# Attention and two MLPs on one core: first output operand split among the last pairs, fourteen early weight loads, batch 1 on the later batches' path

## The chip, the core and the metric

The kernel runs on one core of a Trainium2 chip. The metric is the device time of one execution, in microseconds (us). The core's engines run side by side: PE multiplies matrices, DVE and ACT do elementwise work, POOL and SP here mostly issue DMAs (transfers between DRAM and the on-chip buffers). Each engine works through its own instructions in the order in which they were written, and waits on semaphores for the others.

## What is computed

Cut to what matters (B = 8 batches, 8 heads, 576 positions, head width 64, 32 packed queries; both MLPs are 4608 x 512 -> 2048 -> 512):

```
p_packed = sm_attn(p, k, v)                  # 32 packed queries attend to 576 positions
x = sm_attn(q, p_packed, p_packed)           # 576 positions attend to the 32 packed rows
h = x @ w_in;  g = where(h >= 1, h, where(h <= -1, 0, (h + 1)**2 / 4));  y = g @ w_out
h = y @ w2_in; out = silu(h) @ w2_out
```

## The kernel before, in words

Every large product is made of three matmuls on high and low halves of the operands (`PASSES`), so an operand that PE reads is first cast on ACT (the high half) and subtracted on DVE (the low half). In `pair_split` these are L789 (ACT CAST) and L790 (DVE).

**First half: attention and first MLP.** Each of 8 batches is worked through in 32 steps (16 for each half of its tokens); a step is six matmuls of the first product (L662, `ps_h`), activation work on ACT (L671, L672, L681) and DVE (L677, L687), and twelve matmuls of the second product (L697, `ps_y`). Between the steps stand the attention jobs of the next batch: s1 (scores of the packed queries, lines 272 and 283), pp (the packed rows), s2 (scores of all positions against the packed rows) and wp (the packed rows multiplied into the weights w_in, so that attention and first MLP become one product). Batches 0 and 1 make s2 with 36 matmuls of 64 columns (L417), its maxima and differences straight from PSUM (L428, L430) and its transposes on PE (L454, with an eviction L474 and L476), and wp with 4 matmuls of 64 rows by 512 columns for each of two halves (L563). Batches 2 to 7 pack heads onto smaller array tiles: s2 is 16 matmuls in 64x32 tiles (L486, L497) and its transposes run on DVE (L511 STREAM_TRANSPOSE); wp is 16 matmuls in 64x32 tiles (L575). The raw weights of batch 0 and 1's time are converted on DVE by L156 and L157, `raw` and `w`, beside the steps.

**Second half: second MLP.** It runs in 6 blocks. A block has 56 h units (`h_product`, L829: six matmuls of 128x384 each) and then 56 o units (`o_product`, L881). Products are combined as in Winograd's scheme, 7 products for 8: the h units come in 8 pairs p, seven products j each, and sums of PSUM banks (`c_sum`, L850, DVE) and `c_silu` (L860, ACT) make four results, c11, c12, c21 and c22. When two pairs are there, `t_sum` (L869, DVE) makes the differences t1 to t4. The o units take the operands c11, t2, c21, t3, t1, t4, c22 in that order (`OPERAND`, j = 0 to 6), each in four tiles h = 0 to 3, and `o_split` (through `pair_split`) cuts each tile into halves four units before its first use. The weights of both products, summed beforehand and kept in DRAM, come as one tile of 256 KB a unit (`load_a`, L776, on SP's queue), in a ring of 9 tiles.

**The order.** All is put into one list, `events`, with a number (steps or units) as its key, and is written out sorted by it. `unit_h` and `unit_o` number the units of the second MLP, `bu` puts work behind a unit, and `load_a` for unit n is put 3 units ahead of it for the first nine and 8.6 units ahead for the rest. Before the second MLP starts, the last results of the first one must be stored to DRAM (L712, `y_dram`) and read back in other tiles (L784, `yr`); these transfers share SP's queue with the weights.

## Time and profile before

| what | value |
|---|---|
| median of 3 runs | 1478.59 us (1477.93 to 1478.86) |
| the profiled execution's own time | 1477.16 us |
| its span in the trace | 1475.4 us |
| PE busy | 1448.3 us, 98% of the span |
| DVE, ACT, POOL busy | 966.4, 781.8, 85.1 us |
| granted PE clock, mean | 0.999 |

The span is the time between the first and the last instruction in the trace; 1.76 us of the execution lie around it. In the rows below, an engine's idle time is given with what ended it, as `[0.37 <-DVE g L790]`: 0.37 us, ended by DVE's instruction of line 790 that made a tile g. Tiles are named without their numbers there. PEld is PE's loading of weights, SPq is SP's issuing of DMAs.

### The profile page before, as it was taken

The numbers are of one execution on the slowest core, as the hardware profiler recorded it, in microseconds if no ns is written. First come the engines' busy times: TensorE is split into PE (matmuls) and PEld (weight loads), VectorE is DVE, ScalarE is ACT, GpSimd is POOL, SyncE is SP. The second block draws the span as 40 slices with busy tenths as digits, with TensorE's granted clock in tenths as the row PEclk, the third lists the DMA queues.
The fourth block names the chain that finished last, engine by engine and source line by source line (L and its number), as shares of the span: only waits on it lengthen the run. The fifth ranks groups of instructions, "written<-read, shape, count | busy, mean of one in ns | idle before, by whom it ended". The sixth has DMA issues, their size and how long they took to land.

```text
span 1475.4 us, 28405 instructions
## 1 busy us (share of the span) xinstructions
PE 1448.3 (98%) x10534; PEld 1376.5 (93%) x10534; DVE 966.4 (66%) x1807; ACT 781.8 (53%) x1621; POOL 85.1 (6%) x132
## 2 busy tenths in 40 slices
PE   8999999999999999999999999999999999999998
PEld 6788998989899898999999999999999999999998
DVE  5887576675867758586637756755764774675664
ACT  4776667676676666667643533533542461362342
POOL 1430000000000000000000000000000000000000
PEclk9999999999999999999999999999999999999999
DMA  9563455646464654544338789789789889888886
GB/s 337 184 234 128 158 175 190 220 156 228 157 217 160 198 172 168 202 167 160 112 115 277 239 296 296 238 283 308 240 271 319 251 250 313 268 248 286 251 245 222
DMA packets 196505, 329.82 MB, mean 224 GB/s; under 512 B 30608, under 2 KB 83856, under 8 KB 196368
## 3 DMA queue, kind: packets, MB, share of 16 engines
q1 hardware_dynamic: 186896, 294.98, 61.8%
q0 software_dynamic: 9472, 33.04, 6.5%
q8 instruction: 84, 1.38, 0.4%
q14 instruction: 53, 0.43, 0.1%
HBM read 274.33 MB, written 53.61 MB: 222 GB/s over the span
## 4 chain that ended last, share of the span: by engine, by line
PE 84%; DVE 7%; ACT 2%; issue 1%; DMA 1%; SPq 0%; DVEq 0%; ACTq 0%
PE ps_y L697 24%; PE ps_h L829 23%; PE ps_o L881 21%; PE ps_h L662 12%; PE ps_wp L575 2%; DVE gt L869 1%; PE ps_pp L366 1%; DVE g L790 1%; DVE u L677 1%; DVE g L687 1%; DVE raw L156 1%; ACT g L789 1%; PE ps_wp L563 0%; DVE w L157 0%; PE ps_s L272 0%
## 5 line engine op out<-in xcount | busy, mean ns | idle before, releaser
L697 PE MATMUL ps_y<-g,w_o 128*128 128x288 f32 x3072 | 458.0, 298 | 1.7 <-POOL g L687 1.1
L697 PEld LDWEIGHTS ps_y<-g,w_o 128*128 128x128 f32 x3072 | 420.9, 188 | 33.4 <-ACT u L671 10.1
L881 PE MATMUL ps_o<-g,a2r 128*128 128x384 f32 x2016 | 355.0, 335 | 8.0 <-DVE g L790 8.0
L881 PEld LDWEIGHTS ps_o<-g,a2r 128*128 128x128 f32 x2016 | 348.9, 188 | 13.2 <-DVE g L790 13.2
L829 PE MATMUL ps_h<-y,a2r 128*128 128x384 f32 x2016 | 351.7, 334 | 2.7 <-DMA a2r<-a_dram 2.7
L829 PEld LDWEIGHTS ps_h<-y,a2r 128*128 128x128 f32 x2016 | 349.4, 188 | 3.3 <-issue 2.2
L662 PE MATMUL ps_h<-a,wp 128*128 128x288 f32 x1536 | 245.8, 296 | 2.0 <-DVE u L677 1.1
L677 DVE SCALAR_TENSOR_TENSOR u<-ps_h,u 128x288 f32<-128x288 f32 x256 | 116.1, 455 | 167.3 <-ACT u L672 166.8
L662 PEld LDWEIGHTS ps_h<-a,wp 128*128 128x128 f32 x1536 | 217.7, 188 | 5.9 <-DVE u L677 2.2
L671 ACT ACTIVATE u<-ps_h,half 128x288 f32<-128x288 f32 x256 | 128.2, 501 | 172.9 <-PE ps_h L662 153.7
L860 ACT ACTIVATE gs<-c 128x384 f32<-128x384 f32 x144 | 75.7, 526 | 136.1 <-DVE c L850 136.1
L850 DVE TENSOR_TENSOR c<-ps_h,u 128x384 f32<-128x384 f32 x144 | 79.6, 556 | 60.3 <-PE ps_h L829 50.9
L672 ACT ACTIVATE u<-u 128x288 f32<-128x288 f32 x256 | 113.8, 445 | 8.1
L687 DVE TENSOR_TENSOR g<-u,g 128x288 fp32r<-128x288 f32 x240 | 108.7, 453 | 1.6 <-ACT g L681 1.6
L681 ACT CAST g<-u 128x288 fp32r<-128x288 f32 x256 | 106.7, 417 | 0.5 <-PE ps_y L697 0.3
L790 DVE TENSOR_TENSOR g<-gs,g 128x768 fp32r<-128x768 f32 x96 | 88.4, 952 | 15.7 <-ACT g L789 15.5
L845 ACT COPY p<-ps_h 128x384 f32<-128x384 f32 x48 | 23.1, 482 | 118.6 <-PE ps_h L829 116.1
L789 ACT CAST g<-gs 128x768 fp32r<-128x768 f32 x96 | 75.6, 832 | 12.8 <-PE ps_o L881 9.4
L790 DVE TENSOR_TENSOR g<-gt,g 128x768 fp32r<-128x768 f32 x72 | 65.4, 950 | 0.0
L850 DVE TENSOR_TENSOR os<-ps_o,u 128x384 f32<-128x384 f32 x36 | 19.4, 557 | 65.2 <-PE ps_o L881 65.2
L860 ACT ACTIVATE gs<-ps_h 128x384 f32<-128x384 f32 x48 | 23.5, 492 | 72.3 <-PE ps_h L829 72.3
L913 POOL DMA_DIRECT2D out<-os x40 | 21.5, 540 | 674.4 <-ACT os L906 337.2
(131 smaller groups left out, 1123.1 us busy)
## 6 DMA issues: line engine op xcount, KB each, us to landing
a2r<-a_dram SPq DMA_DIRECT2D x336, 256.0 KB, 3.4
a2r<-o_dram SPq DMA_DIRECT2D x336, 256.0 KB, 3.1
win<-win_dram POOLq DMA_DIRECT2D x48, 512.0 KB, 4.2
raw<-w_in SPq DMA_DIRECT2D x32, 512.0 KB, 7.8
raw<-w_out SPq DMA_DIRECT2D x32, 512.0 KB, 7.2
a_dram<-a2w SPq DMA_DIRECT2D x56, 256.0 KB, 3.1
o_dram<-a2w SPq DMA_DIRECT2D x56, 256.0 KB, 2.7
y_dram<-ysb SPq DMA_DIRECT2D x36, 288.0 KB, 2.5
```

The costliest lines, as they stand in the source:

```text
L662: nc.tensor.matmul(ps[:, :HB], w[:, i, o:o + P], a2[:, k, g, :], start=(n == 0), stop=(n == 3 * NG - 1))
L671: nc.scalar.activation(u, h_ps[s][:, :HB], AF.Relu, bias=half, scale=0.5)
L672: nc.scalar.activation(u, u, AF.Square)
L677: nc.vector.scalar_tensor_tensor(u, h_ps.pop(s)[:, :HB], 1.0, u, op0=ALU.max, op1=ALU.min)
L681: nc.scalar.copy(g[:, 0], u_t[s])
L687: eng.tensor_tensor(g[:, 1], u_t.pop(s), g[:, 0].bitcast(F32), op=ALU.subtract)
L697: nc.tensor.matmul(acc["y"][d][:, :HB], w[:, i, d * P:(d + 1) * P], g[:, k], start=(first and n == 0), stop=(last and n == 2),)
L790: nc.vector.tensor_tensor(lo, src, hi.bitcast(F32), op=ALU.subtract)
L829: nc.tensor.matmul(ps, w[:, x, a * P:(a + 1) * P], b_t[i, j][k][:, a], start=(n == 0 and j in FIRST), stop=(n == 3 * KH - 1), skip_group_c ...
L850: nc.vector.tensor_tensor(t, bk[*key, b][:, :TH], sb[key, other], op=ALU.add)
L860: nc.scalar.activation(gs(*key, name), src, AF.Silu)
L881: nc.tensor.matmul(ps, w[:, x, d * P:(d + 1) * P], g[k][:, p % 2], start=(p == 0 and n == 0 and j in FIRST), stop=(p == NPR - 1 and n == 2 ...
```

## The change

It has three parts.

1. `o_split` of the first operand (j = 0, c11) goes from four units ahead of its use to ten, for h = 0 to 3 less p // 4 (p = 0, 2, 4, 6), that is among the h units of the last pairs. The four `t_sum` of the last pair go behind unit `unit_o(i, 0, 2)` and the three after it, one each. A c11 tile is kept until t1 has been made from it.
2. The first fourteen weight tiles, not nine, come from the big pool, and their loads are written 0.4 units apart from four units ahead of the first h unit.
3. Batch 1 uses the code of batches 2 to 7 in s1, s2, the transposes and wp, with its weights taken from on-chip tiles (`win_t[1, f, g] = w_in_t[g, f]`), and its wp jobs start two steps sooner.

```diff
         def pp_mm(g):
-            vs = [... if b >= 2 and g == 0 else v_t.pop((b, i)) for i in (range(2) if b >= 2 else (g,))]
+            vs = [... if b >= 1 and g == 0 else v_t.pop((b, i)) for i in (range(2) if b >= 1 else (g,))]
...
-                w = win_t[f, j // 2][:, j % 2]
+                w = win_t[b, f, j // 2][:, j % 2]
...
-            ] if b < 2 else [
+            ] if b < 1 else [
                 [J(s1_tiles), J(s1_8), J(s1_end8)],
...
-            [[J(wp, f, g) for g in range(NG)] if b < 2 else [J(wp8, f)], [J(wp_out, f, g) for g in range(NG)]]
+            [[J(wp, f, g) for g in range(NG)] if b < 1 else [J(wp8, f)], [J(wp_out, f, g) for g in range(NG)]]
...
     def store_win(f, g):
+        win_t[1, f, g] = w_in_t[g, f]
         nc.sync.dma_start(win_dram[f, g], w_in_t[g, f])
...
-    RING = 9
+    RING, FIRST_A = 9, 5
...
     def load_a(n, src):
-        if n < RING:
+        if n < RING + FIRST_A:
             t = big.tile([P, 2, KH * P], F32R, tag="big", name="a2r")
...
         nc.vector.tensor_tensor(dst, gs_t[i, h, x], gs_t[i, h, y], op=ALU.subtract)
+        if name == "t1" and (i, 0, h) in go_t:
+            gs_t.pop((i, h, "c11"))
...
     def o_split(i, j, h):
-        go_t[i, j, h] = pair_split(gs_t.pop((i, h, OPERAND[j])), "g2")
+        key = i, h, OPERAND[j]
+        go_t[i, j, h] = pair_split(gs_t[key], "g2")
+        if j or (i, h, "t1") in gs_t:
+            gs_t.pop(key)
...
-    G = dict(pf1=4, pb1=18, w1=2, pf=2, pb=16, ...)
+    G = dict(pf1=4, pb1=18, w1=0, pf=2, pb=16, ...)
...
                 if p % 2:
                     for x, name in enumerate(("t1", "t2", "t3", "t4")):
-                        bu(b + 14 + x // 2, 20 + x % 2, t_sum, i, p // 2, name)
+                        n = unit_o(i, 0, 2) + x if p == NPR - 1 else b + 14 + x // 2
+                        bu(n, 20 + x % 2, t_sum, i, p // 2, name)
...
                     if p % 2 == 0:
-                        bu(n - 4, 5, o_split, i, j, p // 2)
+                        bu(n - (4 if j else 10 - p // 4), 5, o_split, i, j, p // 2)
...
-                ev(K0 + n - (3 if n < RING else RING - 0.4) + 0.39, load_a, n, src)
+                ev(K0 + (n * 0.4 - 4 if n < RING + FIRST_A else n - RING + 0.4) + 0.39, load_a, n, src)
```

In the order's rows below a line stands for one instruction (or as many as "x3" says): line, operation, tile written <- tiles read. Lines of the new kernel are two or three lower than those of the old one.

**DVE where the first block's h units end and its o units begin.** `gs` are results c of two pairs, `gt` differences, `g2` the low halves that the o units read. Of before (gs_10323, gs_10484 and gs_10646 are the c11 tiles h = 1, 2, 3; gt_10286 is t2 of h = 0):

```order
L850 TENSOR_TENSOR c_10722<-ps_h2_10629,u2_10636 128x384
L850 TENSOR_TENSOR c_10734<-ps_h2_10588,u2_10622 128x384
L790 TENSOR_TENSOR g2_10738<-gs_10323,g2_10737 128x768
L850 TENSOR_TENSOR c_10749<-ps_h2_10600,u2_10636 128x384
L790 TENSOR_TENSOR g2_10765<-gs_10484,g2_10764 128x768
L869 TENSOR_TENSOR gt_10776<-gs_10751,gs_10646 128x768
L869 TENSOR_TENSOR gt_10778<-gs_10697,gt_10776 128x768
L790 TENSOR_TENSOR g2_10789<-gs_10646,g2_10788 128x768
L869 TENSOR_TENSOR gs_10751<-gs_10697,gs_10751 128x768
L869 TENSOR_TENSOR gt_10793<-gs_10724,gt_10778 128x768
L790 TENSOR_TENSOR y2_10804<-yr_10158,y2_10803 128x768
L790 TENSOR_TENSOR g2_10816<-gt_10286,g2_10815 128x768
```

And now (gs_10488 and gs_10650 are c11 of h = 2 and 3; gt_10290 is t2 of h = 0):

```order
L848 TENSOR_TENSOR c_10697<-ps_h2_10592,u3_10673 128x384
L848 TENSOR_TENSOR c_10707<-ps_h2_10604,u3_10687 128x384
L788 TENSOR_TENSOR g2_10712<-gs_10488,g2_10711 128x768
L848 TENSOR_TENSOR c_10723<-ps_h2_10619,u2_10626 128x384
L848 TENSOR_TENSOR c_10734<-ps_h2_10633,u2_10640 128x384
L788 TENSOR_TENSOR g2_10739<-gs_10650,g2_10738 128x768
L848 TENSOR_TENSOR c_10750<-ps_h2_10592,u2_10626 128x384
L848 TENSOR_TENSOR c_10761<-ps_h2_10604,u2_10640 128x384
L867 TENSOR_TENSOR gt_10792<-gs_10763,gs_10650 128x768
L788 TENSOR_TENSOR y2_10803<-yr_10164,y2_10802 128x768
L867 TENSOR_TENSOR gt_10806<-gs_10709,gt_10792 128x768
L788 TENSOR_TENSOR g2_10817<-gt_10290,g2_10816 128x768
```

The four splits of c11 now stand ahead of the last sums c, two of them further up than these rows, and the first split of t2 stands behind two of the last pair's differences and not behind four.

**SP where the second MLP starts.** `a2r` are the weight tiles. Of before (a2r_10152 is unit 7's, a2r_10156 unit 13's and a2r_10166 unit 8's):

```order
L776 DMA a2r_10069<-a_dram_100 128x512
L776 DMA a2r_10095<-a_dram_100 128x512
L776 DMA a2r_10099<-a_dram_100 128x512
L776 DMA a2r_10120<-a_dram_100 128x512
L776 DMA a2r_10124<-a_dram_100 128x512
L712 DMA y_dram_99<-ysb_10129 128x2x288
L712 DMA y_dram_99<-ysb_10139 128x2x288
L776 DMA a2r_10152<-a_dram_100 128x512
L776 DMA a2r_10156<-a_dram_100 128x512
L784 DMA yr_10158<-y_dram_99 128x2x384
L776 DMA a2r_10166<-a_dram_100 128x512
L776 DMA a2r_10169<-a_dram_100 128x512
```

And now:

```order
L774 DMA a2r_10021<-a_dram_100 128x512
L774 DMA a2r_10035<-a_dram_100 128x512
L774 DMA a2r_10055<-a_dram_100 128x512
L774 DMA a2r_10059<-a_dram_100 128x512
L774 DMA a2r_10073<-a_dram_100 128x512
L774 DMA a2r_10087<-a_dram_100 128x512
L710 DMA y_dram_99<-ysb_10139 128x2x288
L710 DMA y_dram_99<-ysb_10149 128x2x288
L782 DMA yr_10164<-y_dram_99 128x2x384
L774 DMA a2r_10173<-a_dram_100 128x512
L774 DMA a2r_10183<-a_dram_100 128x512
L774 DMA a2r_10193<-a_dram_100 128x512
```

All fourteen loads stand ahead of the two stores of `y_dram`, and behind the first `yr` follows unit 14's.

**PE at batch 1's first wp.** `ps_wp` and `ps_s2` are PSUM tiles of wp and s2; g_1326 is one of the tokens' second half, g_1152 the last of their first half. Of before:

```order
L697 MATMUL ps_y_1283<-g_1326,w_o_11_1276 128x288 x3
L697 MATMUL ps_y_1284<-g_1326,w_o_11_1276 128x288 x3
L697 MATMUL ps_y_1285<-g_1326,w_o_11_1276 128x288 x3
L697 MATMUL ps_y_1286<-g_1326,w_o_11_1276 128x288 x3
L417 MATMUL ps_s2_1361<-pp1_89,qt_1112 64x64 x16
L563 MATMUL ps_wp_1378<-w_in_0_0_242,pp1_89 64x512 x2
L563 MATMUL ps_wp_1381<-w_in_1_0_309,pp1_89 64x512 x2
L662 MATMUL ps_h_1393<-a2_358,wp_0_3_1166 128x288 x3
L662 MATMUL ps_h_1393<-a2_358,wp_1_3_1161 128x288 x3
```

And now:

```order
L660 MATMUL ps_h_1244<-a2_358,wp_0_3_1180 128x288 x3
L660 MATMUL ps_h_1244<-a2_358,wp_1_3_1175 128x288 x3
L572 MATMUL ps_wp8_1253<-w_in_0_0_242,pp1_89 32x512
L572 MATMUL ps_wp8_1254<-w_in_0_0_242,pp1_89 32x512
L572 MATMUL ps_wp8_1253<-w_in_0_0_242,pp1_89 32x512
L572 MATMUL ps_wp8_1254<-w_in_0_0_242,pp1_89 32x512
L572 MATMUL ps_wp8_1253<-w_in_1_0_309,pp1_89 32x512
L572 MATMUL ps_wp8_1254<-w_in_1_0_309,pp1_89 32x512
L572 MATMUL ps_wp8_1253<-w_in_1_0_309,pp1_89 32x512
L572 MATMUL ps_wp8_1254<-w_in_1_0_309,pp1_89 32x512
L695 MATMUL ps_y_914<-g_1152,w_o_7_812 128x288 x3
L695 MATMUL ps_y_915<-g_1152,w_o_7_812 128x288 x3
```

The first wp has moved from behind the first s2 to ahead of the last step of the tokens' first half, with 20 rows of the tokens' second half now between it and the first s2; it is eight rows, the two banks in turn, in place of two rows of two. DVE follows it there:

```order
L685 TENSOR_TENSOR g_1197<-u_1167,g_1197 128x288
L156 TENSOR_SCALAR raw_949<-raw_949 128x512
L157 SCALAR_TENSOR_TENSOR w_1287<-raw_949 128x512
L675 SCALAR_TENSOR_TENSOR u_1297<-ps_h_1244,u_1297 128x288
L140 TENSOR_TENSOR wp_0_0_1304<-ps_wp8_1253,wp_0_0_1304 128x512
L140 TENSOR_TENSOR wp_1_0_1307<-ps_wp8_1254,wp_1_0_1307 128x512
L685 TENSOR_TENSOR g_1263<-u_1216,g_1263 128x288
L156 TENSOR_SCALAR raw_1171<-raw_1171 128x512
L157 SCALAR_TENSOR_TENSOR w_1330<-raw_1171 128x512
L685 TENSOR_TENSOR g_1357<-u_1219,g_1357 128x288
```

Of before the two `wp` rows stood behind the first s2's maxima and differences (L428, L430):

```order
L156 TENSOR_SCALAR raw_1140<-raw_1140 128x512
L157 SCALAR_TENSOR_TENSOR w_1390<-raw_1140 128x512
L687 TENSOR_TENSOR g_1343<-u_1272,g_1343 128x288
L677 SCALAR_TENSOR_TENSOR u_1400<-ps_h_1333,u_1400 128x288
L428 TENSOR_REDUCE m2_1410<-ps_s2_1361 128x16
L430 TENSOR_TENSOR e2_1412<-ps_s2_1361,m2_1410 128x512
L140 TENSOR_TENSOR wp_0_0_1414<-ps_wp_1378,wp_0_0_1414 128x512
L140 TENSOR_TENSOR wp_1_0_1417<-ps_wp_1381,wp_1_0_1417 128x512
```

The two rows L140 have moved up by ten rows, ahead of three conversions of raw weights. In place of L428 and L430 there are now two STREAM_TRANSPOSE.

## Rows read from the trace of the kernel before

**Rows 1.** The page: shares of the chain that ended last, by engine.
```profile
PE 84%; DVE 7%; ACT 2%; issue 1%; DMA 1%; SPq 0%; DVEq 0%; ACTq 0%
```

**Rows 2.** Waits over the whole span: engine, line, releaser: us, times, longest us.
```profile
PE ps_o L881 <- DVE g L790: 8.0, 12, 1.1
...
PE ps_h L829 <- DMA a2r<-a_dram: 2.7, 2, 1.9
```

**Rows 3.** Chain of waits, second MLP: start us, us, what, matmuls.
```profile
818.31 2.09 PE ps_o L881 x12
...
878.78 58.24 PE ps_h L829 x336
...
997.48 54.09 PE ps_h L829 x312
```

**Rows 4.** Timeline at the second block's boundary: start, us, what [idle before].
```profile
937.51 0.96 DVE L790 TENSOR_TENSOR g<-gs,g 128x768 fp32r<-128x768 f32 x1 [0.85 <-ACT g L789]
938.38 0.55 DVE L850 TENSOR_TENSOR c<-ps_h,u 128x384 f32<-128x384 f32 x1
...
940.25 0.96 DVE L790 TENSOR_TENSOR g<-gs,g 128x768 fp32r<-128x768 f32 x1 [1.31 <-ACT g L789]
...
943.99 2.36 PE L881 MATMUL ps_o<-g,a2r 128*128 128x384 f32 x12 [0.37 <-DVE g L790]
...
946.46 0.95 DVE L790 TENSOR_TENSOR g<-gt,g 128x768 fp32r<-128x768 f32 x1
...
947.47 3.74 PE L881 MATMUL ps_o<-g,a2r 128*128 128x384 f32 x20 [1.12 <-DVE g L790]
```

**Rows 5.** Chain of waits where the second MLP starts: start us, us, what.
```profile
760.97 0.02 issue
...
763.41 4.58 DMA a2r<-a_dram
```

**Rows 6.** Timeline of SP there (the DMA issues).
```profile
760.62 1.17 SPq L712 DMA_DIRECT2D y_dram<-ysb  x2
761.84 0.98 SPq L776 DMA_DIRECT2D a2r<-a_dram  x2
```

**Rows 7.** Timeline of PE through batch 1's jobs.
```profile
108.14 1.37 PE L417 MATMUL ps_s<-pp,qt 128*64 128x64 f32 x29
...
109.52 1.88 PE L563 MATMUL ps_wp<-w_in,pp 128*64 128x512 f32 x7
...
113.45 1.03 PE L662 MATMUL ps_h<-a,wp 128*128 128x288 f32 x6 [0.36 <-DVE e L430]
...
119.09 0.60 PE L454 MATMUL ps_tr<-ident,e 128*128 128x128 f32 x4
```

**Rows 8.** The same jobs of a later batch, timeline of PE.
```profile
195.34 1.09 PE L486 MATMUL ps_s<-qt,pp 64*32 64x512 f32 x16
...
198.94 0.43 PE L497 MATMUL ps_s2e<-qte,pp 128*32 128x64 f32 x16
...
209.06 1.09 PE L575 MATMUL ps_wp<-win,pp 64*32 64x512 f32 x16
```

**Rows 9.** Stretches: start:end, length, busy PE PEld DVE ACT POOL, clock, DMA.
```profile
98.60:113.50 14.90, 13.90 (x119) 12.29 (x117) 14.10 (x21) 9.93 (x22) 6.87 (x6) 1.00 0.68 232
113.50:165.00 51.50, 51.50 (x413) 45.99 (x414) 31.62 (x75) 29.83 (x71) 1.09 (x2) 1.00 0.48 164
253.00:341.00 88.00, 88.00 (x799) 81.11 (x798) 60.42 (x147) 59.76 (x142) 4.75 (x9) 1.00 0.60 202
```

**Rows 10.** Timeline of DVE in batch 1's first stretch.
```profile
104.45 1.60 DVE L157 SCALAR_TENSOR_TENSOR w<-raw 128x512 uint32<-128x512 uint32 x1
...
111.91 0.68 DVE L428 TENSOR_REDUCE m<-ps_s 128x16 f32<-128x512 f32 x1
...
113.22 1.28 DVE L140 TENSOR_TENSOR wp<-ps_wp,wp 128x512 fp32r<-128x512 f32 x2
```

**Rows 11.** Timeline of DVE, the same job of a later batch.
```profile
197.53 1.30 DVE L511 STREAM_TRANSPOSE e<-ps_s 128x512 f32<-128x512 f32 x2
```

More of the change, by code (lines that the diff above doesn't have):

```diff
@@ L214, in load_k, with q_tiles @@
                 kq_t["ke", b] = t
-    def q_tiles(b):
-        if b:
-            return [[(2 * i * P, P), ((2 * i + 1) * P, P)] for i in range(SC // 2)] + [[(SC * P, ST)]]
+    def q_tiles():
         return [x for t in (0, HB) for x in ([(t, P), (t + P, P)], [(t + 2 * P, HB - 2 * P)])]
@@ L231, in load_q @@
     def load_q(b, i):
-        parts = q_tiles(b)[i]
+        parts = q_tiles()[i]
         n = sum(x[1] for x in parts)
@@ L350, in pp_mm @@
         def pp_mm(g):
-            vs = [v_t[b, i] if b >= 2 and g == 0 else v_t.pop((b, i)) for i in (range(2) if b >= 2 else (g,))]
+            vs = [v_t[b, i] if b >= 1 and g == 0 else v_t.pop((b, i)) for i in (range(2) if b >= 1 else (g,))]
             et, ett = st.pop(("eta", g)), st["etb"]
@@ L358, in pp_mm @@
                     rows = slice(h * NP, (h + 1) * NP)
-                    head = 2 * h + g if b >= 2 else h
+                    head = 2 * h + g if b >= 1 else h
                     va, vb = vs[head // 4]
@@ L374, in pp_norm @@
             for g in range(NG):
-                if b >= 2:
+                if b >= 1:
                     nc.vector.memset(t[:, g, 1 - g], 0.0)
@@ L393, in pp_out @@
             ps = st.pop("pptr")[:, :NG * P]
-            if b < 2:
+            if b < 1:
                 nc.vector.tensor_copy(pp.rearrange("p j m -> p (j m)"), ps)
@@ L402, in att_jobs @@
         W2 = NJ * N2
-        tiles = q_tiles(b)
+        tiles = q_tiles()
         def s2(i):
@@ L412, in s2 @@
                     for j in range(NJ):
-                        if b < 2:
+                        if b < 1:
                             dst = ps[r0:r1, c * W2 + j * N2:c * W2 + (j + 1) * N2]
@@ L579, in wp8 @@
             for e in range(2):
-                win_t.pop((f, e))
+                win_t.pop((b, f, e))
                 st["wp", f, e] = banks[e]
@@ L623, in back @@
         def back(every=4, only=None):
-            if b >= 2:
+            if b >= 1:
                 return back8
@@ L641, in store_win, with load_win @@
     def store_win(f, g):
+        win_t[1, f, g] = w_in_t[g, f]
         nc.sync.dma_start(win_dram[f, g], w_in_t[g, f])
-    def load_win(f, g):
+    def load_win(b, f, g):
         t = big.tile([P, 2, FW], F32, tag="big", name="win")
         nc.gpsimd.dma_start(t, win_dram[f, g])
-        win_t[f, g] = t
+        win_t[b, f, g] = t
     h_ps, u_t, g_t, acc, y_t = {}, {}, {}, {}, {}
@@ L913, in o_sum @@
                 eng.dma_start(out[r:r + P, t, i * TH:(i + 1) * TH], sb.pop(((i, 0, d), name)))
-    G = dict(pf1=4, pb1=18, w1=2, pf=2, pb=16, pw=21, lw=3, lk=4, lv=-1, lq=6, ai=34, ad=25, bev=4, oraw=1)
+    G = dict(pf1=4, pb1=18, w1=0, pf=2, pb=16, pw=21, lw=3, lk=4, lv=-1, lq=6, ai=34, ad=25, oraw=1)
     starts = {b: (0,) if b else (0, KF // 2) for b in range(B)}
@@ L1085, in plan_back @@
         def plan_back(b, n):
-            if b >= 2:
-                for g in range(NG + 1):
-                    at(n - G['lq'] + min(g, 1), load_q8, b, g)
-                slots(n, jobs[b][1]())
-                return
-            for i in range(3):
-                at(n - G['lq'] + G['bev'] * i, load_q, b, i)
-            slots(n, jobs[b][1](G['bev']))
+            for g in range(NG + 1):
+                at(n - G['lq'] + min(g, 1), load_q8, b, g)
+            slots(n, jobs[b][1]())
         jobs = {b: att_jobs(b) for b in range(1, B)}
@@ L1098, in attention_then_two_mlps @@
         for f in range(NF):
+            for g in range(NG):
+                at(KF + 4 * f + G['w1'] - 0.05, store_win, f, g)
             slots(KF + 4 * f + G['w1'], jobs[1][2][f])
-            for g in range(NG):
-                at(KF + 4 * f + G['w1'] + 0.05, store_win, f, g)
         for b in range(2, B):
@@ L1108, in attention_then_two_mlps @@
                 for g in range(NG):
-                    at(n - G['lw'], load_win, f, g)
+                    at(n - G['lw'], load_win, b, f, g)
                 slots(n, jobs[b][2][f])
```

## The prediction

> **What bounds the kernel now.** I read the chain of waits first: PE holds 84% of it and DVE 7% [rows 1], so the kernel is bound by PE and what can be won on the second half is the time in which PE stands still. The list of waits names the two places where it does so there: PE waits for the low halves of operands at L790, 8.0 us in 12 cases, and for the first weight tiles, 2.7 us in 2 cases [rows 2]. In the chain a block's h units run 58.24 us without a break, 336 matmuls, or 0.1733 us each and 1.04 us for a unit of six. The o units have as many matmuls of the same shape, yet those of the second block start at 937.02 (878.78 + 58.24) and end at 997.48: 60.46 us [rows 3]. So 2.22 us go at the boundary of a block, and the boundary of the first one reads alike (818.31 to 878.78, 60.47). The first half is bound by PE too in its steady part: a later batch's stretch is 88.00 us with PE busy for 88.00 of them. Batch 1 differs early: from 98.6 to 113.5 PE works 13.90 of 14.90 us and DVE 14.10, so there DVE is the bound; from 113.5 on PE is busy throughout, 51.50 of 51.50, with DVE at 31.62 [rows 9].
>
> **Part 1, the boundary of a block.** Before, DVE takes the second split of c11 at 937.51 and the third at 940.25, and before each it had stood idle for its ACT cast (0.85 and 1.31 us); between them stands one of the last sums (938.38). The fourth comes behind two differences of the last pair, and PE waits for it at 943.99, having been idle for 0.37. Then come two more differences, a split of y, and only then the split of t2's first tile, at 946.46; PE waits again, to 947.47, idle for 1.12 [rows 4]. Those two idles are 1.49 of the 2.22; the rest is matmuls drawn out behind late weight loads, and it goes with them, since it exists only there. The change puts all four splits ahead of the last sums, in time that DVE has: in these seven us it was idle for 0.85 + 1.31. Written out by hand on the rows' durations (0.87 from one DVE instruction of this size to the next, as from 937.51 to 938.38): the last of c11's splits ends at about 937.2 and is needed at 937.02 + 6 units = 943.3. With the last sum and its silu done at 938.75, DVE goes on with t1, a split of y, t2, and the split of t2's first tile, four times 0.87, to 942.2; PE needs it at 937.02 + 8 units = 945.3. The next tile's split stands four instructions further, 945.7, and is needed at 947.4. The smallest slack is 1.7 us. Nothing waits any more, if this holds. What is put behind: sums of c12 come up to 1.2 us later than now; the bank that they read is written again two units (2.08 us) later. The casts on ACT are hidden in the same way.
>
> Six boundaries of 2.22 us make 13.4. The list of waits counts only two cases for each of the six, 8.0 us; drawn-out matmuls are not in it. Bounds: if only the idle goes, with a part of the rest, 10; above 13.4 nothing is to be had. I take 13.4.
>
> **Part 2, the start of the second MLP.** The last matmuls of the first half end at 760.97, and the chain then runs through SP to a weight load of 4.58 us that was issued at 763.41 [rows 5]. SP shows why: the two stores of y_dram at 760.62 wait for the last results, and the loads of units 7 and 8 stand behind them, the first at 761.84 [rows 6]. Four h units were done by then among the last steps; 52 remain, 54.08 us at 1.04, and the o units start at 818.31 [rows 3], 57.34 after 760.97. That is 3.26 lost, 2.73 of it as waits for loads [rows 2]. Now fourteen loads are ahead of the stores, the last of them some ten us ahead of the point where SP stops. Unit 14 is then the first load behind the stores; it stands behind one read of y where unit 8 stood there before. It would be issued at about 762.3 and land by 766.9 (4.58), and is needed ten units after 760.97, at 771.4. Late next is the ring: later loads wait for a tile to be freed, as all through the blocks, where PE did not wait. Gain 3.2; bounds 2 (a late load remains) and 3.3.
>
> **Part 3, batch 1.** On PE, wp was 1.88 us for each of four parts [rows 7] and is 1.09 in a later batch [rows 8]: 4 x 0.79 = 3.2. s2 was 1.38 (108.14 to 109.52) for each of two large tiles and some 0.4 by its share of matmuls for the small one, and its transposes on PE 0.60, 0.60 and 0.3 [rows 7], together 4.7; it becomes 1.09 + 0.43 [rows 8], so 3.2 less. s1 shrinks as well, but in the early stretch in which DVE, ACT and POOL prepare weights; I give nothing for it. Sum on PE: 6.4.
>
> DVE pays. In the stretch from 98.6 to 113.5 it is the bound, and the first wp's eviction, 1.28 us for two [rows 10], which stood behind that stretch, now stands in it, ahead of three conversions. Two transposes of 1.30 [rows 11] take the place of maxima and differences of 1.31 (111.91 to 113.22) as what frees the scores' bank, and are even. So 1.3 go back, and something of 0.1 for a bank held a little longer. After 113.5 DVE has 20 us free in 51.5 [rows 9], and the longer s2 path (the transposes back, 1.30 for each of two large tiles, and some for the small one: about 3 us more on DVE in all) lies beside PE's work. Net 5.0. Bounds: 0, if the stretch takes all, and 6.4, if the eviction is hidden after all. I take 5.0 because the later batches show this same path with PE busy throughout.
>
> A row that speaks against taking it whole: in the DVE-bound stretch a conversion lasts 1.60 us [rows 10] beside POOL's work. The Trainium skill, "TensorEngine Tiling (Array Packing)", section "Performance Considerations", says that tiling speeds up TensorE but not the emptying of PSUM, which may become the bound. By that rule part 3 gives nothing where DVE already is the bound; the later batches' stretch does not bear it out in steady work, and rival A is the case in which it holds here.
>
> **The sum.** 13.4 + 3.2 + 5.0 = 21.6. The profiled execution took 1477.16, so it would take 1455.6; the median of the runs is 1478.59, 1.43 above, so the forecast is 1457.0.
>
> **Rivals.**
> A. Part 3 is swallowed. The first wp (1.09) is put ahead of the last step of the tokens' first half, so that step's results, DVE's copies of them and all conversions behind come about 1.1 later, the eviction adds 1.28, and the longer s2 path, some 3 us more on DVE, falls into the same stretch or presses on it; 0.8 of it fits into DVE's idle time there (14.90 less 14.10). That is 1.1 + 1.28 + 3 - 0.8 = 4.6, with the 0.1 of the bank 4.7; of 6.4 hardly more than 1 is left, and if a conversion or two more meet POOL's work and last 1.60 like the one at 104.45, nothing: 1461 to 1462. For it: DVE at 14.10 of 14.90. Against: PE's 1.09 comes back as the same job shrinks later.
> B. The stall moves on. The four casts wait on ACT behind silu work, the last splits slip behind the sums, and the second operand's splits come as late as before. The idle of 1.12 with its drawn-out part remains, half of 2.22, at six boundaries: 6.7 lost, 1463.7. Against: 1.7 us of smallest slack.
> C. Slower. Splits ahead of the sums hold PSUM banks: each split costs DVE 0.87 and, where its cast isn't ready, up to the 1.31 that a row shows. Four of them put 8.7 us ahead of the last sums; 2.1 are free (two units until a bank is written again), so PE would stand 6.6 in each block's h units. Less the 2.22 won that is 4.4, six times 26.3, less 8.2 from the other parts: 18 slower, 1497. It decides at (21.6 + 3)/6 = 4.1 us of such waiting in a block. Against it: the casts are written ten units ahead of use, with c11 ready long before, and ACT is half idle.
> D. The loads don't come early: their tiles in the big pool are freed late, and the ninth to fourteenth wait on SP in front of the stores. Then part 2 gives nothing and perhaps costs as much: 1460 to 1463. Against: unit 13's tile waits only for a first-half operand used some steps before.
>
> **How the numbers follow.** Forecast 0.64, A 0.14, B 0.11, C 0.03, D 0.08. The forecast's own range goes from 1455.3 (13.4 + 3.3 + 6.4 = 23.1) to about 1460 (losses of two parts at their middle). The range for 8 in 10 takes in A and D and most of B: 1454.5 to 1464. About 0.2%, 3 us, is what a measurement of this kernel can tell from no change; a gain under 3 would need A, B and D at once: 0.01 for the same. Faster 0.96, slower 0.03.
>
> **What would show it.** Part 1: in each o stage of the chain one piece of 336 matmuls in 58.2 us, no wait of L881 for L790; a wait of L829 for L850 would mean C, a remaining one of L881 for L790 at the eighth unit B. Part 2: no wait of L829 for a weight tile, o units starting at about 815 less what came before. Part 3: batch 2's first step 5 us earlier; if DVE grows in the stretch around 100 to 115 and PE's idle there rises above 1.0 to about 6, A. The prediction is wrong if a boundary still takes over 59 us, or if the first half shrinks by less than 3.

## The result, and the profile after

The changed kernel takes 1456.87 us (median of 4 runs, 1456.44 to 1459.14) against 1478.26 us of the kernel before beside it: a ratio of 0.9858, 95% interval 0.9841 to 0.9875. The forecast was 1457.0, in the range 1454.5 to 1464. The profiled execution is the slowest of the four: 1459.14, its span 1457.4; the others' spans were 1454.6 to 1455.2.

The chain of waits of the changed kernel (start us, us, engine and line, matmuls), where the second MLP starts, at two boundaries and in the last block:

```profile
758.78 54.11 PE ps_h L827 x312
812.89 58.24 PE ps_o L884 x336
871.13 58.24 PE ps_h L827 x336
929.37 58.24 PE ps_o L884 x336
...
1395.29 58.26 PE ps_o L884 x336
```

The o stages, 60.46 and 60.47 us in [rows 3], are 58.24 now, one piece of 336 matmuls each. The page's groups of the two products (line, engine, operation, count | busy us, mean ns | idle before) show the same over the whole span, where [rows 2] had 8.0 and 2.7 us:

```profile
L827 PE MATMUL ps_h<-y,a2r 128*128 128x384 f32 x2016 | 351.2, 334 | 0.0
L884 PE MATMUL ps_o<-g,a2r 128*128 128x384 f32 x2016 | 350.4, 334 | 0.0
```

To see where the time went, the span is cut at five places that both kernels have: a pair of L662 steps just ahead of batch 1's s1, the s1 of batch 2, the end of the last step of the first half, the first o unit and the last.

| stretch (us) | before | after | difference | forecast |
|---|---|---|---|---|
| start to the pair of steps ahead of batch 1's s1 | 56.48 | 58.09 | +1.61 | 0 |
| from there to batch 2's s1 | 100.52 | 96.72 | -3.80 | -5.0 |
| to the end of the first half's last step | 603.97 | 603.97 | 0 | 0 |
| to the first o unit | 57.34 | 54.11 | -3.23 | -3.2 |
| to the end of the last o unit | 653.26 | 640.66 | -12.60 | -13.4 |
| to the end of the span | 3.83 | 3.85 | +0.02 | 0 |
| span | 1475.4 | 1457.4 | -18.0 | -21.6 |

The first row is hardly the change's: both kernels issue the same transfers there, and in the fourteen profiles told of here that pair of steps stands between 54.99 and 58.09 us. (The middle one of the seven with the old batch 1 is 55.42, of the seven with the new one 56.12; no run asks whether those 0.7 us belong to the change.) In the changed kernel's profile it was latest of all. A tile of k landed late there: PE's wait of 2.44 us for it ended at 11.41, against one of 1.12 that ended at 10.41 before. Behind that wait the granted clock was 0.59 from 12 to 16 us, where the thirteen other profiles have 1.00, and sixteen filling matmuls took 3.18 us against 2.05. So of the 21.4 us between the medians this pair of profiles shows 19.6 in the three places of the change, and the part on the second MLP's start, under why the prediction was right, says what the rest may be.

At the second block's boundary, the timeline of the changed kernel (start us, us, engine, line, what, [idle before]):

```profile
929.21 15.07 PE L884 MATMUL ps_o<-g,a2r 128*128 128x384 f32 x86
...
931.37 0.96 DVE L867 TENSOR_TENSOR gt<-gs 128x768 f32<-128x768 f32 x1 [0.60 <-ACT gs L858]
...
932.25 0.95 DVE L788 TENSOR_TENSOR y<-yr,y 128x768 fp32r<-128x768 f32 x1
933.12 0.95 DVE L867 TENSOR_TENSOR gt<-gs,gt 128x768 f32<-128x768 f32 x1
933.99 0.95 DVE L788 TENSOR_TENSOR g<-gt,g 128x768 fp32r<-128x768 f32 x1
...
937.46 0.95 DVE L788 TENSOR_TENSOR g<-gt,g 128x768 fp32r<-128x768 f32 x1
```

PE runs through from 929.21. With the o units starting at 929.37, the first split of t2 (933.99) ends 5.6 us behind that start, where the forecast had 5.2 and PE's need was 8.3; the second (937.46) ends at 938.4 and is needed ten units behind the start, at 939.8. The smallest slack is 1.4 us; it was forecast as 1.7. Of the two idles of [rows 4], 0.37 and 1.12, none is left in PE's row.

SP's issues where the second MLP starts, the answer to [rows 6]:

```profile
758.44 1.17 SPq L710 DMA_DIRECT2D y_dram<-ysb  x2
759.66 0.50 SPq L782 DMA_DIRECT2D yr<-y_dram  x1
760.25 1.89 SPq L774 DMA_DIRECT2D a2r<-a_dram  x4
```

No load of the first fourteen is behind the stores now; the four at 760.25 are units 14 to 17.

PE through batch 1's jobs, the answer to [rows 7]:

```profile
100.15 1.09 PE L572 MATMUL ps_wp<-w_in,pp 64*32 64x512 f32 x16
...
108.64 1.73 PE L695 MATMUL ps_y<-g,w_o 128*128 128x288 f32 x11 [1.47 <-DVE g L685]
...
112.68 1.09 PE L483 MATMUL ps_s<-qt,pp 64*32 64x512 f32 x16
...
115.74 0.43 PE L494 MATMUL ps_s2e<-qte,pp 128*32 128x64 f32 x16 [0.98 <-DVE u L675]
...
117.35 1.41 PE L572 MATMUL ps_wp<-w_in,pp 64*32 64x512 f32 x16
```

The jobs are shorter, as [rows 8] had them, but PE now waits for 1.47 and 0.98 us in this stretch where it waited for 0.64 and 0.36 before. Busy time from a later pair of L662 steps, at 81.94 (83.55 after), to batch 2's s1, first before, then after (start:end, length, PE, PEld, DVE, ACT, POOL, clock, DMA share, GB/s):

```profile
81.94:157.00 75.06, 73.81 (x633) 65.40 (x631) 56.44 (x111) 47.66 (x107) 13.63 (x12) 1.00 0.49 168
```

```profile
83.55:154.81 71.26, 68.36 (x615) 60.16 (x613) 57.65 (x121) 47.24 (x108) 13.67 (x12) 1.00 0.53 179
```

PE works 5.45 us less (73.81 to 68.36) and is idle for 1.65 more (1.25 to 2.90): 3.80. Ahead of that later pair, where s1 is packed now, nothing is gained: 25.46 us from pair to pair in both kernels.

### The profile page after: what moved, and what is told of

Same layout as the page of the kernel before. It is cut to its first block, busy times and chain, and to the rows that moved or that the text cites. A ratio compares the mean times of both kernels' runs of the same rounds, so it can differ in the third digit from the quotient of the medians.

```text
span 1457.4 us, 28411 instructions
## 1 busy us (share of the span) xinstructions
PE 1439.0 (99%) x10532; PEld 1373.0 (94%) x10532; DVE 967.1 (66%) x1817; ACT 778.3 (53%) x1622; POOL 84.9 (6%) x132
## 4 chain that ended last, share of the span: by engine, by line
PE 89%; DVE 4%; ACT 1%; issue 1%; DMA 0%; DVEq 0%; ACTq 0%
PE ps_y L695 25%; PE ps_h L827 24%; PE ps_o L884 24%; PE ps_h L660 12%; PE ps_wp L572 2%; PE ps_pp L363 1%; DVE g L685 1%; DVE u L675 0%; DVE raw L156 0%; PE ps_s L269 0%; DVE w L157 0%; PE ps_et L328 0%; PE ps_s L483 0%; DVE wp L140 0%; ACT u L669 0%
## 5 line engine op out<-in xcount | busy, mean ns | idle before, releaser
L884 PE MATMUL ps_o<-g,a2r 128*128 128x384 f32 x2016 | 350.4, 334 | 0.0
L675 DVE SCALAR_TENSOR_TENSOR u<-ps_h,u 128x288 f32<-128x288 f32 x256 | 116.1, 455 | 164.1 <-ACT u L670 163.6
```

The costliest lines, as they stand in the source:

```text
L675: nc.vector.scalar_tensor_tensor(u, h_ps.pop(s)[:, :HB], 1.0, u, op0=ALU.max, op1=ALU.min)
L884: nc.tensor.matmul(ps, w[:, x, d * P:(d + 1) * P], g[k][:, p % 2], start=(p == 0 and n == 0 and j in FIRST), stop=(p == NPR - 1 and n == 2 ...
```

## The experiments

The median of a kernel moves by a microsecond or two from one group of runs to the next (1477.0 to 1478.5 for the kernel before), so where a microsecond matters the stretches of the traces decide.

**Each part alone.** The kernel before with part 1 only:

```diff
...
-                        bu(b + 14 + x // 2, 20 + x % 2, t_sum, i, p // 2, name)
+                        n = unit_o(i, 0, 2) + x if p == NPR - 1 else b + 14 + x // 2
+                        bu(n, 20 + x % 2, t_sum, i, p // 2, name)
...
-                        bu(n - 4, 5, o_split, i, j, p // 2)
+                        bu(n - (4 if j else 10 - p // 4), 5, o_split, i, j, p // 2)
```

(Left out, here and in the runs with one half of part 1, are the lines of `t_sum` and `o_split` that keep a c11 tile until t1 is made.)

> The kernel before with part 1 alone (early splits of c11, late last differences). Theory T (the three parts remove separate stalls and add): each o stage of the chain becomes 58.24 us without a wait of L881 for the low halves, five boundaries give 2.23 us and the last one 1.4 us, so 12.6 us less than before, 1465.6. Rival R (parts depend on each other; the weights that come late at the boundary hold back half of it): a wait for weight tiles stays at the boundary and the gain is 6 to 7 us, 1471 to 1472.

Measured: 1464.2 us, ratio 0.990 (0.9883 to 0.9916). No wait for L790's low halves is left, and a block takes 116.48 us from one h stage to the next, two pieces of 58.24 (877.80 to 994.28). Theory T holds for the place. The median fell by 14.3 us, more than the 12.6 that T sums.

Part 2 only:

```diff
-    RING = 9
+    RING, FIRST_A = 9, 5
...
-        if n < RING:
+        if n < RING + FIRST_A:
...
-                ev(K0 + n - (3 if n < RING else RING - 0.4) + 0.39, load_a, n, src)
+                ev(K0 + (n * 0.4 - 4 if n < RING + FIRST_A else n - RING + 0.4) + 0.39, load_a, n, src)
```

> The kernel before with part 2 alone (fourteen early loads from the big pool). Theory T: no wait for a weight tile at the start of the second MLP, the o units begin 3.2 us sooner, 1475.1. Rival R: without the early splits the time saved is lost again in the first block's boundary, whose splits wait for results and not for weights: under 1 us of gain, 1477.5 to 1478.

Measured: 1472.97 us, ratio 0.9961 (0.9947 to 0.9976). In its chain the h units run through from the last step's end and the first o unit comes 54.12 us later:

```profile
759.84 54.11 PE ps_h L829 x312
813.96 2.08 PE ps_o L881 x12
```

That is T's 3.2 us, and the boundaries keep their full loss (813.96 to 874.43, 60.47), so nothing of it is lost again there. The median fell by 5.5 us, more than the 3.2; see the clock below.

Part 3 only:

```diff
-    G = dict(pf1=4, pb1=18, w1=2, pf=2, ...)
+    G = dict(pf1=4, pb1=18, w1=0, pf=2, ...)
...
-            ] if b < 2 else [
+            ] if b < 1 else [
...
```

> The kernel before with part 3 alone (batch 1 on the later batches' path). Theory T: 5 us less, 1473.3, with the steps of batch 2 starting some 5 us sooner than before, less what the start of the execution differs by. Rival A (the DVE-bound stretch from 98 to 116 us swallows it): 2 us less or nothing, 1476 to 1478.

Measured: 1474.39 us, ratio 0.9966 (0.9954 to 0.9978). From the pair of steps (55.72) to batch 2's s1 (152.46) it takes 96.74 us. That is 3.8 less than before: between T's 5 and rival A's 2, nearer to T. The changed kernel once more gives the same:

> The changed kernel once more, unaltered, as the measure for its variants on the same chip and for how far the early stretch differs between executions. Theory T: from the step at 58.09 (two sets of six matmuls of L660 ahead of batch 1's s1) to batch 2's s1 it takes 96.7 us again, as in the changed kernel's first profile, against 100.5 of before, so part 3 is worth 3.8 us and not 5.0; what stands ahead of that step differs by up to 3 us from execution to execution. Rival: the 96.7 was one execution's and this one shows 95.5 or less, as the predicted 5.0 wants.

```profile
56.26 1.76 PE L660 MATMUL ps_h<-a,wp 128*128 128x288 f32 x12
...
152.90 1.09 PE L269 MATMUL ps_s<-kt,pbd 64*32 64x512 f32 x16
```

96.64 us, with the median at 1456.44 (ratio 0.9852, 0.9836 to 0.9869). The stretch is 100.5 to 100.7 in each of the seven profiles whose batch 1 is as before, and 96.6 to 96.7 in all three whose batch 1 is as changed. So 3.8 is part 3's worth, and T of this run holds. By the medians the three parts alone give 14.3, 5.5 and 4.1 us, 23.9 together against 21.4 of the whole; they come from groups of runs that differ by a microsecond or two, so it is the stretches that show that the parts add.

**Which half of part 1 does it.** Only the early splits (the differences stay):

```diff
...
-                        bu(n - 4, 5, o_split, i, j, p // 2)
+                        bu(n - (4 if j else 10 - p // 4), 5, o_split, i, j, p // 2)
```

> The kernel before with half of part 1: the splits of c11 early, the last pair's differences where they were. Theory T (the early splits do it all; the differences moved behind only widen the slack): from the last sum, 938.75, six DVE instructions of 0.87 end the first split of t2 at 944.0, before the 945.3 at which it is needed; so no wait at a boundary, 58.24 us for each o stage, 12.5 us less than before, as with all of part 1. Rival: the second wait of 1.12 stays since four differences and a split of y stand ahead of t2's split: o stages of 59.6, 5 us less than before.

Measured: 1466.1 us, ratio 0.9915 (0.9901 to 0.993).

```profile
819.07 58.24 PE ps_o L886 x336
877.31 58.24 PE ps_h L829 x336
935.55 58.24 PE ps_o L886 x336
```

Each o stage is 58.24 us: the early splits alone do all that part 1 does there. Only the late differences:

```diff
...
-                        bu(b + 14 + x // 2, 20 + x % 2, t_sum, i, p // 2, name)
+                        n = unit_o(i, 0, 2) + x if p == NPR - 1 else b + 14 + x // 2
+                        bu(n, 20 + x % 2, t_sum, i, p // 2, name)
```

> The kernel before with the other half of part 1: only the last pair's differences later, the splits of c11 four units ahead as before. Theory T: the fourth split of c11 no longer stands behind two differences, so the first wait goes, but t2's splits come as late as before (first near 945.5, second near 949 against the 947.4 at which it is needed), and a wait of 1 to 1.5 us stays at each boundary: o stages of 59.4 to 60, 2 to 5 us less than before in all. Rival (the order of the last differences is the cause and the splits would do where they are): o stages of 58.3, 12 us less.

Measured: 1472.98 us, ratio 0.9966 (0.9953 to 0.9979). In the timeline the wait for the fourth split of c11 has gone, and the second wait stands one tile later, at t2's second split:

```profile
943.36 0.95 DVE L790 TENSOR_TENSOR g<-gt,g 128x768 fp32r<-128x768 f32 x1
...
946.83 2.69 DVE L790 TENSOR_TENSOR g<-gt,g 128x768 fp32r<-128x768 f32 x3
...
947.84 7.38 PE L886 MATMUL ps_o<-g,a2r 128*128 128x384 f32 x41 [1.09 <-DVE g L790]
```

Its o stages are 60.02 us (1054.01 to 1114.03), at the upper end of T's, the last 58.48. The gain by stages is 5 x 0.45 for the first five and 1.2 for the last, 3.4: T, and the rival falls. The late differences alone move the stall, as the forecast's rival B feared for the whole; beside the early splits they are worth nothing that shows.

**How many early loads.** The first nine loads early, the ring as before:

```diff
-                ev(K0 + n - (3 if n < RING else RING - 0.4) + 0.39, load_a, n, src)
+                ev(K0 + (n * 0.4 - 4 if n < RING else n - RING + 0.4) + 0.39, load_a, n, src)
```

> The kernel before with half of part 2: the first nine loads (0.4 units apart, from four units ahead of the first) early, the ring of nine as before, so that units 0 to 12 stand ahead of the stores of y_dram on SP and unit 13 right behind them. Theory T (units 7 and 8 stood behind the stores, that is all): no wait for a weight tile at the start of the second MLP, o units 54.1 us after the last step as with all of part 2, and PE's granted clock stays at 1.00 there; 3 to 5.5 us less than before. Rival (the five further tiles are needed: the ring gets nine units ahead only when it starts full): units 13 to 17 come late, 1 to 3 us are lost again.

Measured: 1472.85 us, ratio 0.997 (0.9958 to 0.9982). The h units run from the last step's end without a wait:

```profile
760.27 49.97 PE ps_h L829 x288
...
874.85 58.24 PE ps_h L829 x336
```

T: the place of units 7 and 8 in SP's row was all. The five further tiles from the big pool bring nothing that these runs can show.

**The first wp of batch 1.** The changed kernel with the eviction alone put back behind the conversions:

```diff
-            slots(KF + 4 * f + G['w1'], jobs[1][2][f])
+            slots(KF + 4 * f + G['w1'], jobs[1][2][f][:1])
+            slots(KF + 4 * f + G['w1'] + (3 if f == 0 else 1), jobs[1][2][f][1:])
```

> The changed kernel, but the eviction of batch 1's first wp (L139 and L140) two steps later, behind the stretch's conversions of raw weights, where it stood before; its matmuls stay early. Theory T (this eviction on DVE in the DVE-bound stretch costs what it lasts, 1.3 us, and the wait for its ACT cast with it): PE's idle time from 100 to 117 falls from 2.6 to about 1.3 us, the time by 1.3 us to 1455.6. Rival B1 (the stretch is bound by the conversions and POOL's work beside them, and the eviction only shifts the idle): no difference beyond 0.5 us, 1456.9. A third possibility: the two PSUM banks of wp are held longer and a later product waits for one, slower by 1 us or more.

Measured: 1460.76 us, ratio 0.9879 (0.9865 to 0.9894); the stretch takes 101.18 us (56.12 to 157.30), 4.5 more than the changed kernel's.

```profile
109.29 1.04 PE L483 MATMUL ps_s<-qt,pp 64*32 64x512 f32 x2 [0.15 <-DVE u L675]
113.32 1.59 PE L483 MATMUL ps_s<-qt,pp 64*32 64x512 f32 x14 [2.99 <-DVE u L675]
115.74 1.81 PE L660 MATMUL ps_h<-a,wp 128*128 128x288 f32 x6 [0.83 <-DVE e L508]
```

s2 wants two banks of PSUM out of a pool of four. The first wp still holds two (its L140 comes at 116.21) and a step's `ps_h` one, so one is free, and after two of its sixteen matmul records s2 waits 2.99 us for the step's bank, which DVE's line 675 frees behind the conversions. The six matmuls at 115.74 take 1.81 us, against 0.96 to 1.06 where the granted clock is 1.00, and the clock (the third figure from the end, as in the stretches above) says why:

```profile
113.00:117.00 4.00, 2.85 (x19) 1.44 (x20) 2.29 (x5) 0.00 (x0) 1.07 (x1) 0.60 0.01 2
117.00:121.00 4.00, 4.00 (x41) 2.31 (x39) 3.19 (x8) 2.32 (x6) 0.00 (x0) 0.55 0.00 0
```

Of the 4.5 us, 1.3 are PE's idle time (0.15 + 2.99 + 0.83 = 3.97 us, against 1.47 + 0.98 + 0.19 = 2.64 in the changed kernel); the rest fits the eight us at a clock of 0.60 and 0.55, in which at most 3.4 us of work were not done. The third possibility came, and T of this run falls. The changed kernel with wp two steps later, matmuls and eviction:

```diff
-    G = dict(pf1=4, pb1=18, w1=0, pf=2, ...)
+    G = dict(pf1=4, pb1=18, w1=2, pf=2, ...)
```

> The changed kernel with batch 1's wp two steps later (w1 = 2 as before the change): matmuls and evictions both stand behind s2 again. Theory T (the eviction in the DVE-bound stretch costs its 1.3 us): the stretch from the step at 58.09 to batch 2's s1 falls from 96.7 to about 95.4, the time by 1.3 us. Rival B2 (PSUM banks: s2's two and wp's two are then all four of that pool, as in the run with the late eviction alone): the next product waits for the transposes on DVE, 98 us or more, 1 to 4 us slower.

Measured: 1459.72 us, ratio 0.9874 (0.9859 to 0.9888); the stretch takes 99.17 us (55.52 to 154.69).

```profile
111.44 1.63 PE L572 MATMUL ps_wp<-w_in,pp 64*32 64x512 f32 x14 [2.38 <-DVE u L675]
...
128.23 1.83 PE L695 MATMUL ps_y<-g,w_o 128*128 128x288 f32 x12 [1.10 <-DVE ysb L702]
```

```profile
111.00:115.00 4.00, 3.56 (x32) 1.90 (x36) 2.88 (x7) 1.74 (x4) 0.23 (x1) 0.61 0.01 3
```

Rival B2: s2 holds two banks and a step's `ps_h` one, wp wants two, and after two of its sixteen records it waits 2.38 us for the step's bank, which L675 frees here too. Here too the clock behind the wait is low, 0.61 for four us, or 1.6 us of work. PE's idle time (the two waits shown) is 3.48, 0.84 above the changed kernel's; the two make the 2.5 us. So without the move ahead of s2 the new path gives 1.4 us, and with it 3.8. The first wp one step sooner still:

```diff
-                at(KF + 4 * f + G['w1'] - 0.05, store_win, f, g)
-            slots(KF + 4 * f + G['w1'], jobs[1][2][f])
+                at(KF + 4 * f + G['w1'] - 0.05 - (f == 0), store_win, f, g)
+            slots(KF + 4 * f + G['w1'] - (f == 0), jobs[1][2][f])
```

> The changed kernel with batch 1's first wp, matmuls and eviction, one step sooner, where DVE still waits for ACT and PE between its instructions. Theory T (the eviction in the DVE-bound stretch and the ACT casts that it queues behind cost the 1.47 us that PE waits for L685 there): that wait falls below 0.5, from the step at 56 to batch 2's s1 it takes 95.3 to 95.8 us in place of 96.7, the time is 1 to 1.4 us lower. Rival (the bound is the sum of DVE's and POOL's conversions in the stretch): the wait reappears at the next step or at L494, 96.5 us or more, no difference.

Measured: 1455.67 us, ratio 0.9853 (0.9837 to 0.987); the stretch takes 95.86 us (56.71 to 152.57).

```profile
113.51 0.43 PE L494 MATMUL ps_s2e<-qte,pp 128*32 128x64 f32 x16 [1.80 <-DVE u L675]
114.13 1.06 PE L660 MATMUL ps_h<-a,wp 128*128 128x288 f32 x6 [0.19 <-DVE e L508]
```

The wait of 1.47 is gone, and L494's wait has grown from 0.98 to 1.80. So the eviction did cost, but more than half of what its removal frees is taken back at L675 behind the conversions: 0.8 us of 1.47 to 1.5 remains. Both expectations are half right. By the stretch it is the shortest kernel of these; by the ratios it can't be told from the changed one.

**What wp's share is.** The changed kernel with batch 1's wp by the old matmuls:

```diff
-            [[J(wp, f, g) for g in range(NG)] if b < 1 else [J(wp8, f)], [J(wp_out, f, g) for g in range(NG)]]
+            [[J(wp, f, g) for g in range(NG)] if b < 2 else [J(wp8, f)], [J(wp_out, f, g) for g in range(NG)]]
```

> The changed kernel with batch 1's wp by the old matmuls (L560, whole columns, as in batch 0) and all else as changed; the rows of wp come in another order than s2's there, so the output isn't the reference's. Theory T (as the prediction summed it: wp's packing is half of PE's saving, 0.79 us for each of four): from the step at 56 to batch 2's s1 99.4 to 99.9 us in place of 96.7, the time 2.7 to 3.2 us above the changed kernel's. Rival (in that stretch DVE is the bound, and the first one or two wp are hidden by it): 98.3 or less, 1.6 us or less.

Measured: 1459.56 us, ratio 0.988 (0.9866 to 0.9895); the stretch takes 99.73 us (55.50 to 155.23), 3.0 more than the changed kernel's 96.7, with the same waits in it (1.47, 0.98). T: wp's packing gives the forecast's 3.2 nearly whole.

**The kernel before once more.**

> The kernel before, unaltered, for one profile more. Theory T (at the start of the second MLP PE's granted clock falls in those executions in which PE has waited some 2.1 us or more in one piece for unit 8's weights, and holds where it waited 2.0 or less; a fall costs 1.8 us): whichever wait this execution has, the clock in the four us behind it follows that line, and the h units behind it take 51.7 us with a fall, 50.0 to 50.2 without. From the step at 56 to batch 2's s1 100.5 to 100.6. Rival: no such link; a fall without a wait of 2.1, or the reverse.

Measured: 1478.15 us. The four us behind the wait for unit 8's weights (start:end, length, PE, PEld, DVE, ACT, POOL, granted clock, DMA share, GB/s) in this profile, in the first one of before, and in two of the runs above whose loads were as before:

```profile
768.00:772.00 4.00, 4.00 (x16) 4.00 (x16) 1.07 (x2) 0.52 (x1) 0.00 (x0) 0.63 0.37 139
```

```profile
768.00:772.00 4.00, 3.87 (x22) 3.90 (x23) 1.57 (x3) 1.05 (x2) 0.00 (x0) 1.00 0.81 291
```

```profile
768.00:772.00 4.00, 4.00 (x15) 4.00 (x15) 1.12 (x2) 0.56 (x2) 0.00 (x0) 0.58 0.63 237
```

```profile
768.00:772.00 4.00, 4.00 (x25) 4.00 (x24) 1.83 (x4) 1.58 (x3) 0.00 (x0) 1.00 0.72 241
```

And the wait itself in the same four profiles:

```profile
767.57 4.59 PE L829 MATMUL ps_h<-y,a2r 128*128 128x384 f32 x16 [2.68 <-DMA a2r<-a_dram]
```

```profile
768.13 4.08 PE L829 MATMUL ps_h<-y,a2r 128*128 128x384 f32 x22 [1.89 <-DMA a2r<-a_dram]
```

```profile
767.83 4.40 PE L829 MATMUL ps_h<-y,a2r 128*128 128x384 f32 x15 [2.41 <-DMA a2r<-a_dram]
```

```profile
767.31 4.95 PE L829 MATMUL ps_h<-y,a2r 128*128 128x384 f32 x27 [2.00 <-DMA a2r<-a_dram]
```

Two of them have a clock of 0.63 and 0.58, two have 1.00. Where it fell, the 288 matmuls behind the wait took 51.7 us, else 50.2. This execution had the longest wait of all and a fall, as theory T had it; the two other profiles with that wait (part 3 alone, early splits only) had a fall as well, to 0.67 and 0.60.

The length of that wait alone isn't what decides, though. Earlier in the same executions, near 34 us, PE waits once for a tile of q. In this profile and in that of the first wp one step sooner (the waits, then the four us behind each):

```profile
33.52 2.40 PE L417 MATMUL ps_s<-pp,qt 128*64 128x64 f32 x32 [1.91 <-DMA qt<-qT]
35.58 1.51 PE L414 MATMUL ps_s<-pp,qt 128*64 128x64 f32 x32 [2.65 <-DMA qt<-qT]
```

```profile
34.00:38.00 4.00, 4.00 (x45) 3.71 (x44) 3.16 (x5) 2.55 (x6) 2.62 (x3) 0.61 1.06 370
36.00:40.00 4.00, 3.49 (x49) 3.03 (x47) 3.14 (x6) 2.77 (x7) 2.62 (x3) 1.00 1.07 324
```

The shorter wait has a fall behind it and the longer one none. Waits of 2.28 and 2.49 us had none either (the unpacked wp, wp behind s2), while 2.00 and 2.05 had one (early splits only, part 2 alone, part 3 alone). So theory T's line fits the six profiles at the second MLP's start, and the rival holds elsewhere.

## Why the prediction was right, and where its terms were off

The time came out as forecast, and each part removed the stall that it was to remove. Two terms were too large, and something not in the sum made up for them: that the median came within 0.2 us of the forecast is luck, for the three stretches show 19.6 us of the 21.6. Neither sign of being wrong came: a boundary takes 58.24 us and not over 59, and the first half shrank by 3.8 us in its stretch (2.2 in this profile as a whole, with its late start). Three sums of the prediction are a little off, without weight for the range: six times 2.22 is 13.3, 23.1 off gives 1455.5, and in rival A 1.7 us are left of 6.4.

**Part 1.** Mechanism and place right: 58.24 us a stage, no wait. The term was mis-sized in "six boundaries of 2.22". The last block has no next block, so no splits of y stand between its last differences and t2's split; its o stage took 59.65 us before and lost only 1.4. Five times 2.23 and 1.4 are 12.6, as measured. The working also booked the gain to the whole of part 1; the half that moves the splits does it alone. Rivals B and C did not come: the slack of 1.7 was 1.4, and no h unit waited for a bank.

**Part 2.** 3.2 forecast, 3.23 in the traces. What the step did not see is the granted clock. In four of six profiles with the late loads PE's clock fell behind the wait, for a further 1.5 us (51.7 us against 50.2 for 288 matmuls); before's profile, on which the sum was made, is one of the two in which it held. The loads' stall thus costs 3.2 us in some executions and about 5 in others, where the wait was longer too (from the first half's last step to the first o unit 57.3 us in before's first profile, 59.7 in its second), and part 2 removes both. Rival D did not come: with the early loads no wait for a weight tile is left there. This would explain why part 2 alone moved the median by 5.5. The second pair of profiles, before once more against the changed kernel once more, has such an execution of before in it, and there the three places give 4.01, 5.59 and 12.61, 22.2 together; the 21.4 of the medians lie between the two pairs. The executions behind the medians have no traces, so that this is what filled the gap is argued, not shown.

**Part 3.** 5.0 forecast, 3.8 measured, three times over. Of its terms, wp's 3.2 was 3.0. PE's saving in all was 6.4 in the forecast and 5.45 by the busy times, so it is s2 with its transposes that was mis-sized, 3.2 for some 2.4: the forecast compared the jobs' busy times as the rows list them, and what stands beside the packed jobs is not in these rows. (The y products are part of it: by busy time they take 40.69 us in that stretch before, 41.06 after and 41.01 with the old wp.) The idle that DVE gives back was 1.4 in the forecast and 1.65 in the trace. But the step was wrong in its direction: it booked the first wp's early eviction as the price of the move, as if 6.4 were to be had without it. The runs show that the move is most of the gain: with wp behind s2, two jobs and a step's product want five banks of four, PE waits 2.4 us for one, the clock falls behind that wait, and 1.4 us of gain are left. (The eviction has its price too: one step sooner gave 0.8 us more.) The bank that the working counted at 0.1 us was the term that mattered. Rival A, the stretch that takes all, was wrong in size: PE's idle there rose by 1.65 and not by 5. What the Trainium skill says in "TensorEngine Tiling (Array Packing)", section "Performance Considerations", of the emptying of PSUM as a possible bound behind faster matmuls, shows here in part: in those 1.65 us, where L140's and L675's emptying of PSUM stands among the conversions, and as the banks in the runs with wp later. It didn't take the gain.

**Open.** Where the rest of the 0.8 us of s2's saving went was not looked for by a run of its own. Nor was it tried to move the conversions of raw weights out of that stretch, which the run with the first wp sooner names as what is late next.

## What to carry to other kernels

When an operand's preparation is late at a stage's boundary, first move the part that is ready early (here the splits of c11) and leave the rest where it is; count the boundaries one by one, for the last one has other work around it. Where a job is made shorter on PE, write down which PSUM banks it and its neighbours hold at that point: moving the wp jobs by two steps cost 2.5 us here, nearly what packing all four of them gave (3.0). And take a stall's price from more than one profile, since the clock behind it may differ from execution to execution.

## What the runs showed of the hardware that was not expected

The granted clock can fall behind a wait of PE, and the fall adds a loss of its own: 1.5 us where unit 8's weights were late, some 1.6 and up to 3.4 us behind the two waits for a bank. Where unit 8's weights were late, the clock of the next four us was 0.58 to 0.67 in four profiles and 1.00 in two; these are means between the two levels of 1.2 and 2.4 GHz, so PE ran a part of that time at the lower. PE had waited 0.80 to 0.96 us and, after six matmuls, 2.10, 2.17, 2.41 and 2.68 us in the four, and 0.84 and 1.89, 0.86 and 2.00 in the two. Behind the waits of 2.99 and 2.38 us for a PSUM bank it was 0.55 to 0.61 over eight and four us. Behind the waits at the block boundaries, 0.37 and 1.12 us [rows 4], and behind those of 1.47 and 0.98 in the changed kernel's batch 1 it stayed at 1.00. Near 34 us it held behind waits of 2.28, 2.49 and 2.65 us and fell in the eleven other profiles, whose waits there were 1.91 to 3.33. These executions make no rule for when it falls; they show that a stall can bring a second loss, and that one execution's trace may not have it.
